# One product per column: TENSOR_TENSOR replaced by TENSOR_SCALAR with a scalar per partition, in the exponential's bias of an attention and feed-forward kernel

## The chip, the core and the metric

The kernel runs on one core of a Trainium2 chip. The metric is the time of one execution in microseconds (us) of the device; lower is better. Engines are named as the profile names them: PE (TensorE, matrix products; its weight loads are PEld), DVE (VectorE), ACT (ScalarE), POOL (GpSimd), SP (the queue from which this kernel starts its DMAs).

## What is computed

Attention with a hash mask, and a feed-forward layer on its result. Cut to what matters:

```
q, k, v: (4, 8, 768, 64);  proj: (64, 6);  w_in: (512, 2048);  w_out: (2048, 512)
q_bucket, k_bucket = 6 sign bits of q @ proj and k @ proj, as a number
scores = where(q_bucket == k_bucket, q @ k.T / 8, -1e9)
attn   = softmax(scores)                       # per row of 768 keys
x      = (attn @ v), heads side by side        # (3072, 512)
h      = x @ w_in
out    = (h * tanh(softplus(h))) @ w_out       # float32, (3072, 512)
```

## The kernel before

The attention is cut into 96 **slots**. A slot takes two heads and 128 queries. Its steps, with the lines of the program:

- **S** (PE, L802): eight matmuls write the scores of both heads into one PSUM tile `ps_s`, 128 x 1536. There is one such tile, so the matmuls of the next slot wait until both exponentials of this slot have read it. The hash codes ride along in the operands, so that a matching pair's score is raised by a large amount.
- **max** (DVE, `scale()`, L809 to L815): a TENSOR_REDUCE (L809) writes the negated maximum of each head's row, two columns, to `svb[:, 0]`. A TENSOR_SCALAR (L812) compares it with a constant and multiplies with a scale per query, which lies in `smalls`: the exponential's scale, `svb[:, 1]`. A TENSOR_TENSOR (L815) multiplies the two: the exponential's bias, `svb[:, 2]`. `svb` and `smalls` lie in SBUF. L812 and L815 come in two versions: both columns in one instruction ("two-wide", 128x2), or each column in its own ("column by column", 128x1 twice).
- **exp** (ACT, L825): one ACTIVATE per head, 128x768, from `ps_s` to `pb` with that head's bias and scale, and the row's sum by the accumulator. When ACT changes its function, an ACT_TABLE_LOAD stands ahead.
- **back**: the sums are made ready (L841 on DVE or POOL, or L838 on ACT), a reciprocal follows (L847, DVE), then the weights are split into a high half (`hl`, L365 on POOL, L367 on ACT or L368 on DVE) and a low half (L386 on DVE, or L392 and L393 on POOL), and DMAs turn them into `PT` (L427).
- **V** (PE, L882): the weights times `v`, into a PSUM tile `ps_t`, which the hash bits and the statistics share (L666, L451, L452; DVE reads them at L670 and L456).

Between the slots stand the feed-forward's matmuls (L913 to L915 with `w_in`, L951 to L953 with `w_out`), ACT's Mish (L931) and its split (L365, L367, L368, L386 on `ffb`), and the preparation of q, k, v and the weights, most of which lies in the first third.

The order of all steps is written out: a list of numbers, `ORDER`, says in which order the steps are issued, and a letter behind a number which version of a step is taken. Every engine works through its own instructions in this order. For the step `max`, 47 slots take the two-wide version and 49 the one column by column. Each of these steps is one version as a whole:

```
op("max", [("DVE", 2200, lambda: scale(False)), ("DVE", 2300, lambda: scale(True))],
   ["ps0", "ps1", f"{sgn}.{j}"], [f"{x}.m0", f"{x}.m1", f"{x}.sc", f"{x}.bi"])
```

Of the kernel before, what the change touches and what calls it, by code (L numbers as in the profile page):

```python
# [15 lines left out]
ALU = mybir.AluOpType  # L16
# [21 lines left out]
class Plan:  # L38
# [3 lines left out]
    def op(self, name, alts, reads=(), writes=(), kind=None, bb=False, after=(), takes=None, frees=None, soft=()):  # L42


        o = Op()
        o.name, o.alts, o.n = name, alts, len(self.ops)
        preds = set(after)
        for regions, write in ((reads, False), (writes, True)):
            for r in regions:
                key, lo, hi = r if isinstance(r, tuple) else (r, 0, 1)  # L50
                for q, a, b, w in self.seen.get(key, ()):
                    if a < hi and lo < b and (w or write) and q is not o:
                        preds.add(q)
        for regions, write in ((reads, False), (writes, True)):
            for r in regions:
                key, lo, hi = r if isinstance(r, tuple) else (r, 0, 1)
                known = self.seen.setdefault(key, [])
                if write:
                    known[:] = [k for k in known if not (lo <= k[1] and k[2] <= hi)]
                known.append((o, lo, hi, write))  # L60
        o.preds = preds
        self.ops.append(o)
        return o
# [173 lines left out]
def lsh_attention_mish_ffn(  # L237
# [10 lines left out]
    nc = tc.nc  # L248
# [18 lines left out]
    op = plan.op  # L267
# [104 lines left out]
    def copied(dst, src, n, engines=("POOL", "ACT", "DVE")):  # L372
# [9 lines left out]
                                                                   op0=ALU.mult)))], [UNIT], [MINUS])  # L382
# [404 lines left out]
    def slot_of(n):  # L787
        u, i = divmod(n, SLOTS)
        j, s = divmod(i, 2)
        return u, u // NU, j, s  # L790

    def att_front(n):

        u, b, j, s = slot_of(n)
        sv, x = svb[:, n % NSV], f"sv{n % NSV}"
        sg, sgn = SIG[u]
        def pe():
            for hh in range(2):
                qi = (2 * j + hh) * 2 + s
                for sl in range(2):  # L800
                    for c0, c1 in ((0, 4), (4, NCH)) if hh == 0 else ((0, 2), (2, NCH)):
                        nc.tensor.matmul(ps_s[:, hh * S + c0 * P:hh * S + c1 * P], QTb[:, u % 2, sl, qi],  # L802
                                         KTb[:, j, sl, hh * NCH + c0:hh * NCH + c1].rearrange("p c t -> p (c t)"),
                                         start=(sl == 0), stop=(sl == 1))
        op(f"S{n}", [("PE", 1300, pe)], [f"QT{u % 2}.0", f"QT{u % 2}.1", f"KT{j}.0", f"KT{j}.1"], ["ps0", "ps1"],
           bb=True)

        def scale(single):
            nc.vector.tensor_reduce(out=sv[:, 0], in_=ps_s.rearrange("p (h e) -> p h e", h=2), axis=AX.X, op=ALU.max,  # L809
                                    negate=True)  # L810
            for w in (slice(0, 1), slice(1, 2)) if single else (slice(0, 2),):
                nc.vector.tensor_scalar(out=sv[:, 1, w], in0=sv[:, 0, w], scalar1=HALF, scalar2=sg[:, j:j + 1],  # L812
                                        op0=ALU.is_le, op1=ALU.mult)
            for w in (slice(0, 1), slice(1, 2)) if single else (slice(0, 2),):
                nc.vector.tensor_tensor(out=sv[:, 2, w], in0=sv[:, 0, w], in1=sv[:, 1, w], op=ALU.mult)  # L815
        op("max", [("DVE", 2200, lambda: scale(False)), ("DVE", 2300, lambda: scale(True))],
           ["ps0", "ps1", f"{sgn}.{j}"], [f"{x}.m0", f"{x}.m1", f"{x}.sc", f"{x}.bi"])

# [275 lines left out]
```

## Time and profile before

| | |
|---|---|
| time, median of 3 runs | 875.53 us (875.09 to 877.47) |
| the profiled execution: its own time, its span | 878.32 us, 876.5 us |
| PE busy | 803.2 us (92%) |
| DVE busy | 695.7 us (79%) |
| ACT busy | 597.0 us (68%) |
| POOL busy | 280.6 us (32%) |

The span reaches from the first instruction to the last. Busy shares are means over the span; the stretches differ. An engine that is idle for most of a stretch can still be the one that the others wait for.

### The profile page before, as it was taken

What the parts mean: (1) busy time and instruction counts of PE and PEld (TensorE: products, weight loads), DVE (VectorE), ACT (ScalarE), POOL (GpSimd) and SP (SyncE); (2) the same over time, 40 slices, a digit from 0 to 9 for tenths busy, and PEclk for the clock granted to TensorE, in tenths of its full rate; (3) what the DMA queues carried; (4) which work ended last, traced back from release to release, by engine and by line L of the source; (5) the groups of instructions that cost most, each with busy time, mean ns of one, the idle gap of its engine ahead of it and who ended that gap; (6) DMA issues with size and microseconds to landing.
All of it is one profiled execution on the core that took longest, in us unless ns stands there. A gap on an engine that the chain in (4) does not pass through costs nothing.

```text
span 876.5 us, 17009 instructions
## 1 busy us (share of the span) xinstructions
PE 803.2 (92%) x6530; PEld 536.5 (61%) x6530; DVE 695.7 (79%) x1344; ACT 597.0 (68%) x947; POOL 280.6 (32%) x260
## 2 busy tenths in 40 slices
PE   2676679899999999999999999999999999999998
PEld 1343347566666767666656766666665766776665
DVE  4697999999899887788889879879888777676412
ACT  5587889878786667668777766567876756657411
POOL 4226443134146433443223212133413143351000
PEclk9697999999999999999999999999999999999999
DMA  9999989589999797688999966899997866556400
GB/s 279 268 243 235 215 195 224 155 187 196 200 172 173 146 186 123 132 156 169 211 188 192 175 122 117 150 178 182 230 161 143 154 120 129 101 98 128 78 25 25
DMA packets 432689, 143.73 MB, mean 164 GB/s; under 512 B 402912, under 2 KB 423392, under 8 KB 432608
## 3 DMA queue, kind: packets, MB, share of 16 engines
q1 hardware_dynamic: 432608, 142.65, 80.9%
q8 instruction: 51, 0.84, 0.4%
q14 instruction: 30, 0.25, 0.1%
HBM read 35.65 MB, written 6.29 MB: 48 GB/s over the span
## 4 chain that ended last, share of the span: by engine, by line
PE 58%; DVE 23%; DMA 8%; ACT 6%; issue 4%; SPq 1%; ACTq 0%; DVEq 0%
PE ps_s L802 10%; PE ps_t L882 8%; DVE svb L809 7%; PE ps_acc L913 7%; PE ps_o L951 6%; PE ps_acc L915 6%; PE ps_acc L914 6%; PE ps_o L953 6%; PE ps_o L952 6%; ACT pb L825 3%; DMA QT<-tok 3%; DVE hl L386 3%; DVE svb L812 1%; DVE ffb L386 1%; DVE svb L815 1%
## 5 line engine op out<-in xcount | busy, mean ns | idle before, releaser
L825 ACT ACTIVATE pb<-ps_s,svb 128x768 f32<-128x768 f32 x192 | 188.8, 986 | 100.9 <-DVE svb L815 84.5
L913 PE MATMUL ps_acc<-X,wi 128*128 128x256 f16 x768 | 209.8, 273 | 0.5 <-ACT ffb L931 0.5
L914 PE MATMUL ps_acc<-X,wi 128*128 128x256 f16 x768 | 209.6, 273 | 0.0
L915 PE MATMUL ps_acc<-X,wi 128*128 128x256 f16 x768 | 209.6, 273 | 0.0
L809 DVE TENSOR_REDUCE svb<-ps_s 128x2 f32<-128x1536 f32 x96 | 168.3, 1753 | 40.6 <-PE ps_s L802 39.4
L386 DVE SCALAR_TENSOR_TENSOR hl<-pb,svb,hl 128x768 f16<-128x768 f32 x146 | 155.8, 1075 | 3.3 <-POOL hl L365 2.7
L802 PE MATMUL ps_s<-KT,QT 128*128 128x512 f16 (+1 forms) x768 | 146.1, 335 | 10.3 <-ACT pb L825 9.7
L953 PE MATMUL ps_o<-wo,ffb 128*128 128x512 f16 x384 | 145.7, 379 | 0.3 <-DVE ffb L386 0.3
L951 PE MATMUL ps_o<-wo,ffb 128*128 128x512 f16 x384 | 145.7, 379 | 0.0
L952 PE MATMUL ps_o<-wo,ffb 128*128 128x512 f16 x384 | 145.7, 379 | 0.0
L365 POOL TENSOR_SCALAR hl<-pb,svb 128x768 f16<-128x768 f32 x66 | 65.3, 990 | 169.8 <-DVE svb L847 73.2
L882 PE MATMUL ps_t<-PT,VT 128*64 128x256 f16 x1728 | 107.6, 280 | 10.9 <-DVE hw L456 4.2
L802 PEld LDWEIGHTS <-QT 128*128 128x128 f16 x768 | 74.2, 99 | 67.2 <-issue 24.1
L882 PEld LDWEIGHTS <-VT 128*64 128x64 f16 x1728 | 94.5, 113 | 29.4 <-issue 23.8
L931 ACT ACTIVATE ffb<-ps_acc,smalls 128x512 f32<-128x512 f32 x96 | 63.5, 684 | 56.0 <-PE ps_acc L915 51.6
L367 ACT ACTIVATE hl<-pb,svb 128x768 f16<-128x768 f32 x77 | 70.9, 929 | 34.1 <-DMA PT<-hl 17.2
L386 DVE SCALAR_TENSOR_TENSOR ffb<-ffb,smalls 128x512 f16<-128x512 f32 x96 | 77.1, 813 | 14.5 <-POOL ffb L365 10.9
L392 POOL TENSOR_SCALAR pb<-pb,svb 128x768 f32<-128x768 f32 x42 | 44.6, 1062 | 136.0 <-ACT hl L367 40.3
L914 PEld LDWEIGHTS <-wi 128*128 128x128 f16 x768 | 75.2, 98 | 14.3 <-issue 1.1
L913 PEld LDWEIGHTS <-wi 128*128 128x128 f16 x768 | 75.1, 98 | 13.1 <-issue 1.4
L915 PEld LDWEIGHTS <-wi 128*128 128x128 f16 x768 | 75.1, 98 | 8.9
L393 POOL TENSOR_TENSOR hl<-pb,hl 128x768 f16<-128x768 f32 x42 | 70.8, 1686 | 3.5
(172 smaller groups left out, 1015.9 us busy)
## 6 DMA issues: line engine op xcount, KB each, us to landing
out_dram<-ffb SPq DMA_DIRECT2D x24, 256.0 KB, 2.8
stg<-in_k_dram SPq DMA_DIRECT2D x12, 384.0 KB, 4.1
stg<-in_v_dram SPq DMA_DIRECT2D x12, 384.0 KB, 4.1
stg<-in_q_dram SPq DMA_DIRECT2D x9, 512.0 KB, 4.9
wi<-in_moe_w_in_dram SPq DMA_DIRECT2D x7, 512.0 KB, 4.9
wo<-in_moe_w_in_dram SPq DMA_DIRECT2D x6, 512.0 KB, 5.1
stg<-in_moe_w_out_dram SPq DMA_DIRECT2D x6, 512.0 KB, 4.7
PT<-hl SPq DMA_TRANSPOSE x192, 4.0
```

The costliest lines, as they stand in the source:

```text
L367: ACT=lambda: nc.scalar.activation(dst, src, AF.Copy, scale=sc),
L386: return [("DVE", 215 + 1.035 * n, port(lambda: nc.vector.scalar_tensor_tensor(out=dst, in0=src, scalar=sc, in1=hi, op0=ALU.mult, op1=ALU. ...
L802: nc.tensor.matmul(ps_s[:, hh * S + c0 * P:hh * S + c1 * P], QTb[:, u % 2, sl, qi], KTb[:, j, sl, hh * NCH + c0:hh * NCH + c1].rearrange(" ...
L809: nc.vector.tensor_reduce(out=sv[:, 0], in_=ps_s.rearrange("p (h e) -> p h e", h=2), axis=AX.X, op=ALU.max, negate=True)
L825: EXP[n, hh] = op("exp", [("ACT", 1075, lambda hh=hh, t=t: nc.scalar.activation(pb[:, t], ps_s[:, hh * S:(hh + 1) * S], AF.Exp, bias=sv[:, ...
L882: nc.tensor.matmul(pv[hh * D:(hh + 1) * D, 0:256], vt[:, w, hh * NCH + c], pt[:, hh, a * NCH + c].rearrange("p s t -> p (s t)"), start=(x ...
L913: nc.tensor.matmul(o, wh, X[:, 0, c], start=(c == 0), stop=False)
L914: nc.tensor.matmul(o, wh, X[:, 1, c], start=False, stop=False)
L915: nc.tensor.matmul(o, wl, X[:, 0, c], start=False, stop=(c == NCC - 1))
L951: nc.tensor.matmul(PS[f"o{s}"], gh, wo[:, g, 0, f2], start=first, stop=False)
L952: nc.tensor.matmul(PS[f"o{s}"], gh, wo[:, g, 1, f2], start=False, stop=False)
L953: nc.tensor.matmul(PS[f"o{s}"], gl, wo[:, g, 0, f2], start=False, stop=last)
```

## The change

In the version column by column, the bias of one column is made by a TENSOR_SCALAR whose tensor operand is the negated maximum and whose scalar operand, one value per partition, is the scale. Before, it was a TENSOR_TENSOR of the two. The two-wide version keeps its TENSOR_TENSOR. The list of the order and the letters in it are unchanged: on every engine the same steps stand in the same places, and on DVE the 98 instructions of the 49 slots column by column are of another kind.

```diff
             for w in (slice(0, 1), slice(1, 2)) if single else (slice(0, 2),):
                 nc.vector.tensor_scalar(out=sv[:, 1, w], in0=sv[:, 0, w], scalar1=HALF, scalar2=sg[:, j:j + 1],
                                         op0=ALU.is_le, op1=ALU.mult)
-            for w in (slice(0, 1), slice(1, 2)) if single else (slice(0, 2),):
-                nc.vector.tensor_tensor(out=sv[:, 2, w], in0=sv[:, 0, w], in1=sv[:, 1, w], op=ALU.mult)
+            if single:
+                for w in range(2):
+                    nc.vector.tensor_scalar(out=sv[:, 2, w:w + 1], in0=sv[:, 0, w:w + 1], scalar1=sv[:, 1, w:w + 1],
+                                            scalar2=None, op0=ALU.mult)
+            else:
+                nc.vector.tensor_tensor(out=sv[:, 2], in0=sv[:, 0], in1=sv[:, 1], op=ALU.mult)
```

## Rows read from the trace of the kernel before

**Rows 1.** Stretches: us, PE, PEld, DVE, ACT, POOL busy (instructions), clock, DMA, GB/s.
```profile
40.00:131.00 91.00, 64.28 (x397) 36.12 (x395) 81.60 (x170) 74.56 (x117) 38.86 (x33) 0.90 0.99 226
131.00:876.50 745.50, 722.67 (x6038) 491.62 (x6038) 591.92 (x1120) 500.99 (x791) 228.75 (x211) 1.00 0.78 151
```

**Rows 2.** Groups by line and shape, DVE: busy us, mean ns | idle before.
```profile
L815 DVE TENSOR_TENSOR svb<-svb 128x1 f32<-128x1 f32 x98 | 26.1, 296 | 0.0
L812 DVE TENSOR_SCALAR svb<-svb,smalls 128x1 f32<-128x1 f32 x98 | 16.4, 209 | 1.7
L812 DVE TENSOR_SCALAR svb<-svb,smalls 128x2 f32<-128x2 f32 x47 | 14.9, 318 | 1.7
...
L841 DVE TENSOR_SCALAR svb<-svb 128x1 f32<-128x1 f32 x60 | 7.3, 147 | 16.4 <-ACT pb L825 16.4
```

**Rows 3.** Timeline, DVE and POOL, three slots: start us, us (joined if touching).
```profile
519.21 1.64 POOL L393 TENSOR_TENSOR hl<-pb,hl 128x768 f16<-128x768 f32 x1
520.84 0.34 DVE L812 TENSOR_SCALAR svb<-svb,smalls 128x1 f32<-128x1 f32 x2
521.09 0.28 DVE L815 TENSOR_TENSOR svb<-svb 128x1 f32<-128x1 f32 x2
...
392.30 1.64 POOL L393 TENSOR_TENSOR hl<-pb,hl 128x768 f16<-128x768 f32 x1
392.84 1.19 DVE L815 TENSOR_TENSOR svb<-svb 128x1 f32<-128x1 f32 x2
...
575.86 0.94 DVE L815 TENSOR_TENSOR svb<-svb 128x1 f32<-128x1 f32 x2
```

**Rows 4.** The chain that ended last, in order of time: start us, us, what.
```profile
41.81 0.92 DVE svb L815 x2
...
82.23 0.54 DVE svb L815 x2
...
89.98 0.20 DVE svb L815 x2
...
96.17 0.62 DVE svb L815 x2
...
149.35 0.53 DVE svb L815 x2
...
254.27 0.80 DVE svb L815 x2
...
392.92 1.11 DVE svb L815 x2
...
777.31 1.03 DVE svb L815 x2
```

**Rows 5.** Timeline of PE at four places: start us, us, [idle before <-releaser].
```profile
254.40 0.38 PE L952 MATMUL ps_o<-wo,ffb 128*128 128x512 f16 x1
254.62 0.38 PE L953 MATMUL ps_o<-wo,ffb 128*128 128x512 f16 x1
255.35 0.18 PE L451 MATMUL ps_t<-smalls,ones 128*128 128x1 bf16 x1 [0.35 <-DVE hsum L670]
...
395.66 0.27 PE L914 MATMUL ps_acc<-X,wi 128*128 128x256 f16 x1
395.77 0.27 PE L915 MATMUL ps_acc<-X,wi 128*128 128x256 f16 x1
396.18 0.38 PE L802 MATMUL ps_s<-KT,QT 128*128 128x512 f16 x1
...
576.29 0.38 PE L953 MATMUL ps_o<-wo,ffb 128*128 128x512 f16 x1
577.07 0.38 PE L882 MATMUL ps_t<-PT,VT 128*64 128x256 f16 x3 [0.40 <-DVE hsum L670]
...
780.11 0.27 PE L915 MATMUL ps_acc<-X,wi 128*128 128x256 f16 x1
780.46 0.38 PE L802 MATMUL ps_s<-KT,QT 128*128 128x512 f16 x1
```

## The prediction

> **What bounds the kernel now.** I read the stretches first [rows 1]. From 131 us to the end PE is busy 722.67 of 745.5 us. All that any change can win there, without touching PE's own work, is the 22.8 us that PE is idle, plus what hides inside PE's modelled ends. From 40 to 131 us it is another picture: PE is busy 64.28 of 91 us and DVE 81.60, so DVE and what hangs on it set the pace, and time won on DVE can become time won.
>
> Then the groups [rows 2]. The column-wise products of L815 take 296 ns in the mean, the column-wise scales of L812, an instruction of the same size with more in it, 209 ns. The timeline says why [rows 3]. At 521.09 POOL's L393 has just ended (519.21 + 1.64 = 520.85), and the two products take 0.28 us together. At 392.84 they take 1.19 us: POOL's L393 began at 392.30 and ends at 393.94, and the products end right behind it, at 394.03. The product stands behind a POOL instruction that began earlier. The reader is to see that no wait on a semaphore shows this; it lies inside the instruction's duration. Where a pair is stretched, a POOL instruction lies across its start or its middle. With some 158 ns as the product's own time (the 0.28 us pair, whose two overlap by some 40 ns, gives about that), the 98 products carry 98 x (296 - 158) = 13.5 us of such waits.
>
> Last the chain that ended last [rows 4], to see which of these waits lie on it. An undisturbed pair shows there with 0.20 us (89.98; the rest of it overlaps the scales). Anything above 0.20 is a wait.
>
> **The change part by part.** *Removed: the wait behind POOL.* The column-wise scale of L812 is already what the product becomes: a TENSOR_SCALAR on one column with a scalar per partition from SBUF. Its mean of 209 ns over 98 instructions, in the very slots in which the product behind it waits, leaves no room for waits of 0.3 to 0.9 us [rows 2]. So I take the wait as gone.
>
> *Added: a dearer instruction.* The new product was not run before. Bounds: 147 ns from below (L841 column-wise, no scalar per partition), 209 ns from above (L812 column-wise, with one) [rows 2]. I take the upper, since the scalar per partition is what the two share. In pairs this is 0.34 us against 0.28 [rows 3], so 0.06 us more per slot; the lower end would make it about nothing. Over 49 slots that is at most 2.9 us of DVE time against 13.5 us of waits removed.
>
> *What of this lies on the path.* I go through the slots on the chain. New pair: 0.20 + 0.06 = 0.26 us.
>
> Before 131 us, where PE has gaps of microseconds, the chain's rows count whole: 82.23 gives 0.54 - 0.26 = 0.28 us, 96.17 gives 0.62 - 0.26 = 0.36 us. In both, DVE's next instruction reads PSUM, so DVE moves up at once. The pair at 41.81 with 0.92 us gives nothing in my sum: DVE's next instruction is a wide TENSOR_SCALAR on SBUF (L368) that I expect to stand behind the same POOL instruction, so that the wait only changes its owner. Four more slots on the chain (at 49, 133, 315 and 466 us) have such a follower, L368 or L386 close behind, and count nothing either.
>
> At 149.35 the chain stays on DVE until long waits of PE some 20 us on: 0.53 - 0.26 = 0.27 us.
>
> After that PE's gap caps what a slot can give, since PE goes on with its own queue. A gap is read from start to start, less the usual step (0.22 us for 512 columns, 0.11 for 256) [rows 5]:
>
> - slot at 254.27: 0.80 - 0.26 = 0.54 us free; PE lost 255.35 - 254.62 - 0.22 = 0.51. Taken: 0.51.
> - slot at 392.92: 1.11 - 0.26 = 0.85 free; PE lost 396.18 - 395.77 - 0.11 = 0.30. Taken: 0.30.
> - slot at 575.86: pair 0.94 against 0.34 [rows 3], 0.60 free; PE lost 577.07 - 576.29 - 0.22 = 0.56. Taken: 0.56.
> - slot at 777.31: 1.03 - 0.26 = 0.77 free; PE lost 780.46 - 780.11 - 0.11 = 0.24. Taken: 0.24.
>
> Sum of the gains: 0.28 + 0.36 + 0.27 + 0.51 + 0.30 + 0.56 + 0.24 = 2.52 us. Against it stand seven column-wise slots on the chain that wait for no POOL instruction, like the one at 89.98: 7 x 0.06 = 0.42 us. The net is 2.1 us off the span, 876.5 to 874.4. All other stalls, the larger part of the 13.5 us, lie where ACT or PE is busy with other work when the bias comes, and that work hides them today: their removal costs and brings nothing.
>
> The profiled execution took 878.32 us, 2.8 more than the median of the runs; I carry the difference over: 875.53 - 2.1 = 873.4 us.
>
> **The rivals.** *More is won than the caps allow.* Exponentials that start earlier bring everything behind them forward, transposes and POOL's halves too, and so also gaps that PE has for other reasons. Without the caps the seven slots give 0.28 + 0.36 + 0.27 + 0.54 + 0.85 + 0.60 + 0.77 = 3.67 us, less 0.42: 3.25, or 872.3 us. If the five slots with a follower that uses POOL's path paid too, at most 0.92 - 0.26 = 0.66 each, it would be 6.5 us, 869.0. For it speaks that DVE is busy 90% from 40 to 131 us; against it, that PE's 722.67 us later leave so little.
>
> *The gain is given back.* PE's gaps are also ended by others (DMAs, ACT's table loads), and a gap that loses one cause can keep its length by the next. Then little is left: 875.5 us. For it speaks that the seven gains are small, 0.24 to 0.56 us, less than one exponential of ACT; against it, that in [rows 5] the releaser at two of four places is DVE's instruction directly behind the pair.
>
> *The change doesn't do what it says: the new product waits too.* For it speaks that a TENSOR_SCALAR can wait: the two-wide L812 takes 318 ns in the mean [rows 2], half as much again as the column-wise one. Against it speaks the column-wise L812 with 209. Then only the price remains, 0.06 us on the some 20 column-wise slots of the chain: 1.2 us, 876.7. The Trainium skill speaks for this rival in its page "SBUF — State Buffer", section "Who interferes with whom": it counts `tensor_scalar` among the operations that can enter a two-port mode and are then shut out while GpSimd works. The same section exempts an instruction with at most one SBUF input outside those modes; by that rule, the trace agrees for one column, with 209 ns.
>
> *Slower: the turn is lost.* Today the short product queues behind POOL and, when it has had its turn, DVE's next instruction follows at once. After the change a long one (L386 or L368 on 768 columns) may ask instead, or start just ahead of POOL's next instruction and hold that one up. Place: the slots whose follower is L386 or L368. Price: POOL's instruction, up to 1.64 us [rows 3], waits for most of one DVE instruction, or the reverse; I take 0.9 us. It decides from six such turns on the path, 5.4 us, which outweigh the 2.1 and add 3.3: 878.8 us. For it speaks that five slots on the chain have such a follower; against it, that the same contest takes place today, one instruction later.
>
> **How the numbers follow.** Chances: forecast 0.50, more is won 0.25, given back 0.10, product waits too 0.07, turn lost 0.08. The runs of this kernel can tell about 0.3%, 2.6 us, from no change: faster means under 872.9 us, slower over 878.2. The forecast's own range is 872 to 875, of which about a quarter (0.12) falls under 872.9. So faster 0.25 + 0.12 = 0.37; slower 0.08 and 0.02 from the run-to-run spread of the others, 0.10; within 0.53. Low end: 870.3, which takes in most of the rival with more gain and leaves out its far end; high end: 876.8, which holds the product that waits too. What is left out is about 0.08 below and 0.09 above.
>
> **What would show it.** The line of the column-wise product should have 98 instructions of about 205 ns, none over 0.3 us, and the DVE instructions behind it should take some of the waits: the means of L368 and L386 on `hl` rise a little. DVE's busy time falls by 5 to 10 us, less than 13.5. PE's waits for the hash sums (L670) near 255 and 577 us vanish. PE's gaps ahead of S that follow two-wide slots stay. The prediction is wrong if the product still shows durations near a microsecond; if the chain's DVE rows vanish but PE's idle time after 131 us doesn't fall by about 1.5 us; or if POOL's durations rise and its halves come late.

## The result and the profile after

The changed kernel takes 870.02 us (median of 13 runs, 868.58 to 874.25) against 875.53 (13 runs): 0.9934 of the time before, 95% interval 0.9921 to 0.9948. That is 5.5 us faster where 2.1 were forecast, and just below the range (870.3). The two profiled executions stand further apart, 868.58 against 878.32 us, than the medians: some of what differs between them is chance, and a second profile of either kernel was taken to tell it apart (below).

The groups by line and shape of VectorE after the change (columns as in [rows 2]). The product is now L816, the two-wide one L819:

```profile
L386 DVE SCALAR_TENSOR_TENSOR hl<-pb,svb,hl 128x768 f16<-128x768 f32 x146 | 157.6, 1088 | 4.3 <-POOL hl L365 3.2 <-ACT hl L367 0.5
...
L368 DVE TENSOR_SCALAR hl<-pb,svb 128x768 f16<-128x768 f32 x49 | 35.7, 728 | 4.5 <-DMA PT<-hl 3.7
...
L812 DVE TENSOR_SCALAR svb<-svb,smalls 128x1 f32<-128x1 f32 x98 | 16.4, 209 | 1.7
L816 DVE TENSOR_SCALAR svb<-svb 128x1 f32<-128x1 f32 x98 | 16.3, 208 | 0.0
```

The product takes 208 ns where it took 296 [rows 2], as much as the scale ahead of it (209): no wait behind POOL is left in it, and its price is the upper bound of the forecast. That it was POOL can be counted: before, 28 of the 98 products take more than 0.25 us, each with a POOL instruction running when it begins; after, 54 of the 98 begin while POOL goes on for at least another 0.15 us, and the longest takes 214 ns. All DVE work together is 8.1 us less (687.6 against 695.7). The product's own line fell from 26.1 to 16.3 us, and L386 and L368 on `hl` took 3.3 us over; their means rose as said (1075 to 1088 and 697 to 728 ns).

PE at the four places of [rows 5], from the timeline after the change (start us, us):

```profile
249.22 0.38 PE L957 MATMUL ps_o<-wo,ffb 128*128 128x512 f16 x1
249.43 0.17 PE L451 MATMUL ps_t<-smalls,ones 128*128 128x1 bf16 x1
...
389.25 0.27 PE L919 MATMUL ps_acc<-X,wi 128*128 128x256 f16 x1
389.36 0.70 PE L802 MATMUL ps_s<-KT,QT 128*128 128x512 f16 x3
...
567.83 0.38 PE L957 MATMUL ps_o<-wo,ffb 128*128 128x512 f16 x1
568.13 0.52 PE L886 MATMUL ps_t<-PT,VT 128*64 128x256 f16 x6
...
770.66 0.27 PE L919 MATMUL ps_acc<-X,wi 128*128 128x256 f16 x1
770.77 0.70 PE L802 MATMUL ps_s<-KT,QT 128*128 128x512 f16 x3
```

Three gaps are gone; at the third place 568.13 - 567.83 - 0.22 = 0.08 us are left of 0.56. These four steps of the forecast came out as written. Most of what was missed lies earlier. This is VectorE and POOL behind slot 8 (slots are numbered from 0; it starts at 94.04 us before), first in the kernel before:

```profile
96.97 1.22 DVE L561 SCALAR_TENSOR_TENSOR wi<-wo,wi 128x1024 int32<-128x1024 int32 x1
98.10 1.40 DVE L368 TENSOR_SCALAR ffb<-ffb,smalls 128x128 f32<-128x128 f32 x1
99.36 1.00 DVE L386 SCALAR_TENSOR_TENSOR hl<-pb,svb,hl 128x768 f16<-128x768 f32 x1
...
98.08 1.34 POOL L546 TENSOR_SCALAR stg<-stg 128x1024 bf16<-128x1024 int16 x1 [1.37 <-ACT pb L825]
```

and in the changed one:

```profile
93.33 0.33 DVE L816 TENSOR_SCALAR svb<-svb 128x1 f32<-128x1 f32 x2
...
93.83 1.21 DVE L561 SCALAR_TENSOR_TENSOR wi<-wo,wi 128x1024 int32<-128x1024 int32 x1
94.96 0.28 DVE L368 TENSOR_SCALAR ffb<-ffb,smalls 128x128 f32<-128x128 f32 x1
95.16 1.01 DVE L386 SCALAR_TENSOR_TENSOR hl<-pb,svb,hl 128x768 f16<-128x768 f32 x1
...
95.32 2.07 POOL L546 TENSOR_SCALAR stg<-stg 128x1024 bf16<-128x1024 int16 x1 [1.37 <-ACT pb L829]
```

Before, L368 began 0.02 us after POOL's L546 and lasted 1.40 us, to POOL's end. After, it begins 0.36 us ahead of L546 and lasts 0.28; the L386 behind it begins ahead of L546 too, by 0.16 us, and now POOL waits, 2.07 against 1.34 us. From L368 to the L386 behind it are 1.26 us before and 0.20 after: 1.06 us, on top of the 0.36 that the pair itself gave. The turn changed hands.

### The profile page after: what moved, and what is told of

Read it like the earlier page. It is cut to its first block, busy times and chain, and to the rows that moved or that the text cites. A ratio compares the mean times of both kernels' runs of the same rounds, so it can differ in the third digit from the quotient of the medians.

```text
span 866.8 us, 17009 instructions
## 1 busy us (share of the span) xinstructions
PE 801.1 (92%) x6530; PEld 534.5 (62%) x6530; DVE 687.6 (79%) x1344; ACT 596.8 (69%) x947; POOL 283.1 (33%) x260
## 4 chain that ended last, share of the span: by engine, by line
PE 65%; DVE 17%; DMA 8%; ACT 5%; issue 3%; POOL 1%; SPq 0%; DVEq 0%; ACTq 0%; POOLq 0%
PE ps_s L802 11%; PE ps_t L886 8%; PE ps_acc L917 8%; PE ps_acc L918 8%; PE ps_acc L919 8%; PE ps_o L955 7%; PE ps_o L957 7%; PE ps_o L956 7%; DVE svb L809 5%; ACT pb L829 3%; DVE hl L386 3%; DMA QT<-tok 2%; DMA PT<-hl 2%; PE ps_l L414 1%; DVE ffb L386 1%
## 5 line engine op out<-in xcount | busy, mean ns | idle before, releaser
L809 DVE TENSOR_REDUCE svb<-ps_s 128x2 f32<-128x1536 f32 x96 | 168.2, 1752 | 41.6 <-PE ps_s L802 40.7
L386 DVE SCALAR_TENSOR_TENSOR hl<-pb,svb,hl 128x768 f16<-128x768 f32 x146 | 157.6, 1088 | 4.3 <-POOL hl L365 3.2
L365 POOL TENSOR_SCALAR hl<-pb,svb 128x768 f16<-128x768 f32 x66 | 64.4, 977 | 169.7 <-DVE svb L851 77.6
L886 PE MATMUL ps_t<-PT,VT 128*64 128x256 f16 x1728 | 105.3, 276 | 7.3 <-DMA PT<-hl 3.7
L886 PEld LDWEIGHTS <-VT 128*64 128x64 f16 x1728 | 92.2, 111 | 25.4 <-issue 20.2
L367 ACT ACTIVATE hl<-pb,svb 128x768 f16<-128x768 f32 x77 | 70.9, 930 | 36.0 <-DMA PT<-hl 17.2
L386 DVE SCALAR_TENSOR_TENSOR ffb<-ffb,smalls 128x512 f16<-128x512 f32 x96 | 78.1, 823 | 15.0 <-POOL ffb L365 11.4
```

The costliest lines, as they stand in the source:

```text
L386: return [("DVE", 215 + 1.035 * n, port(lambda: nc.vector.scalar_tensor_tensor(out=dst, in0=src, scalar=sc, in1=hi, op0=ALU.mult, op1=ALU. ...
L886: nc.tensor.matmul(pv[hh * D:(hh + 1) * D, 0:256], vt[:, w, hh * NCH + c], pt[:, hh, a * NCH + c].rearrange("p s t -> p (s t)"), start=(x ...
```

## The experiments

Each run was timed in turn with the kernel before on the same chip; three were executed once, for a profile. The slot starts that follow are the starts of L809 in each profile. The edits to the changed kernel are conditions on the slot `n`:

```diff
-            if single:
+            if single and CONDITION:          # else the old products
```

**Early and late apart.** Conditions `n <= 12` and `n > 12`.

> The new product only in the ten column-wise slots up to slot 12 (before about 131 us); the old product in the 39 later ones. Theory A (the forecast's sum: only what the chain's rows show is won): 0.6 us from the slots at 82 and 96 us less 0.1 for the price, so 0.5 us less than before, no difference that can be measured. Theory B (the early stretch is bound by VectorE and what hangs on it, so waits there are won with what they trigger; in the two profiles slot 12 starts 5.2 us earlier): 3 to 5 us less than before. Theory C (the two profiled executions differ by chance in the early stretch, where the DMA engines are busy 99%): the start of slot 12 scatters by some us between executions of one kernel, and this run is within 1.5 us of before.

> The new product only in the 39 column-wise slots after slot 12; the old one in the ten early slots. Theory A: the four capped gaps (0.51, 0.30, 0.56, 0.24) and 0.27 at slot 14, less the price, 1.5 us less than before. Theory B: the same or little more, 1.5 to 2.5 us less. Theory D (the later gaps give more than the forecast's caps, as the two profiles say: 4.4 us between slot 12 and the end): 4 us less than before.

Early: 0.9974 (0.996 to 0.9989), 874.53 us; the kernel before, beside these four runs, 875.89. Late: 0.997 (0.9958 to 0.9982), 873.38. So by the ratios the early part is worth 2.3 us (1.0 to 3.5) and the late part 2.6 (1.6 to 3.7). The forecast's sum had 1.5 for the late slots, just below that interval, and 0.5 for the early ones, outside it; theory D's 4 us for the late slots lies outside as well. One of the early kernel's twelve executions, the profiled one, took 2,888 us; it is left out of the ratio (without it the median is 874.24), and the early profile read here is a later one.

**The slots of the sum, and all others.** Conditions `n in (6, 8, 14, 25, 43, 66, 91)` and its opposite.

> The new product only in the seven slots that the forecast's sum counts (6, 8, 14, 25, 43, 66, 91). Theory A: all of the gain and none of the price elsewhere, 2.5 us less than before. Rival: the other slots carry as much (theirs are the five with a follower on POOL's path, and those off the chain), then this has half of the measured 5.5 us or less, and the complement the other half.

> The complement: the new product in the 42 other column-wise slots, the old one in the seven. Theory A: only the price, 0 to 0.4 us more than before. Rival (waits off the chain of before, or in front of a follower that uses POOL's path, pay too): 2 to 3.5 us less than before.

The seven: 0.9964 (0.9949 to 0.998), 872.42 us. The 42 others: 0.9993 (0.9982 to 1.0005), 875.54, no difference. So the forecast chose the right slots. By itself, the relief of 42 slots brings nothing that can be measured, as the forecast said; only the size of the seven was short, 3.2 us against 2.5. Together the two come to 0.43% of the 0.66%; the rest may be spread of the runs or an effect of both together, which these runs can't separate.

**What is chance.** Both kernels once more, and the early one.

> The kernel before once more, for a second profiled execution. Theory C (chance in the early stretch): the start of slot 12 lies 1 to 3 us away from the first one's 131.16. Theory B: it lies within 0.5 us of it, and the first V (near 82.9 us) again runs at half the granted clock and takes 3.4 to 3.5 us. Both: near 445 us PE's wait of 1.1 us for ACT's square of the next tokens is absent (it is absent in all four profiles taken since, of kernels with and without the new product there), so that the span is about 2 us shorter than 876.5.

> The changed kernel once more, for a second profiled execution. Theory B: slot 12 starts at 125 to 127 us again and the first V runs at the full granted clock, 2.2 us. Theory C: slot 12 starts anywhere between 126 and 130 us. Both: the four capped gaps near 247, 389, 567 and 772 us close as in the first profile, so that slots 26, 44, 67 and 92 start 0.5, 0.3, 0.5 and 0.2 us nearer to the slots before them than in the kernel before.

> The new product in the ten slots up to slot 12 only, for a profile of it. Theory B: slot 12 starts as in the changed kernel, 4 to 5 us earlier than in the kernel before, and the steps at slots 26, 44, 67 and 92 are absent. Theory C: slot 12 starts 0.5 to 2 us earlier.

Single executions: 877.06, 872.55 and 871.31 us. The table is worked out from the slot starts of these profiles, of those before and of those on slot 8 below: the time from slot to slot, us.

```
slots from to         8-9    9-12   25-26  43-44  66-67  91-92   start of 12
before                8.30   28.82   7.36   6.95   6.85   6.77   131.16
before, again         8.32   28.78   7.35   6.96   6.86   6.77   129.63
late slots only       8.30   28.81   6.83   6.66   6.38   6.54   131.09
all but the seven     8.31   28.81   7.36   6.95   6.90   6.77   129.59
all but slot 8        8.33   28.85   6.83   6.66   6.38   6.54   130.35
slot 8 held up        8.40   28.87   6.83   6.66   6.38   6.54   129.50
slot 8 only           8.18   27.64   7.36   7.03   6.87   6.78   129.98
the seven             7.48   27.63   6.83   6.66   6.38   6.54   128.41
early slots only      7.22   26.68   7.36   7.08   6.85   6.78   126.06
changed               6.89   27.76   6.83   6.66   6.38   6.54   125.94
changed, again        6.90   27.96   6.83   6.66   6.38   6.54   128.20
```

Two things are to be read here. The four late steps repeat to about a tenth in every profile: where the slot ahead has the new product, 0.53, 0.29, 0.47 and 0.23 us are gone (forecast: 0.51, 0.30, 0.56, 0.24), and elsewhere they aren't. And wherever slot 8 has the new product and isn't held up, the stretch from slot 9 to 12 is 0.9 to 2.1 us shorter and most often also the one from 8 to 9. Theory C is half right: the start of slot 12 scatters by 1.6 us among the kernels with the old product in slot 8 and by 2.3 between the two profiles of the changed one, so of the 5.2 us between the first two profiles a part is chance. Theory B fits the early kernel (slot 12 at 126.06) but not the second profile of the changed one, and that profile shows where most of this scatter sits: the first V, behind slot 6, takes 3.51 us there at a mean granted clock of 0.59, against 2.16 at 1.00 in the first profile, and slot 7 follows slot 6 after 7.70 us instead of 6.19. My guess for the second profile of before was right on the wait near 445 us, which is absent, but wrong on what follows: slot 50 follows slot 48 after 19.40 us there, at a mean granted clock of 0.93, after 19.09 in the first profile, at 1.00, and after 17.7 to 18.9 in the others; the span is 1.2 us shorter, not 2.

**Slot 8 by itself.** Conditions `n == 8` and `n != 8`; and the changed kernel with slot 8 held up ahead of its product:

```diff
+            if n == 8:
+                for w in (slice(0, 1), slice(1, 2), slice(0, 1), slice(1, 2)):
+                    nc.vector.tensor_scalar(out=sv[:, 1, w], in0=sv[:, 0, w], scalar1=HALF, scalar2=sg[:, j:j + 1],
+                                            op0=ALU.is_le, op1=ALU.mult)
             if single:
```

> The new product in slot 8 alone. Theory E (the turn): in the kernel before, VectorE's L368 behind slot 8 asks for POOL's path 0.03 us after POOL's L546 has begun and waits 1.12 us; with the new product it asks 0.35 us ahead and POOL waits instead. Then slot 9 starts 1.2 to 1.4 us nearer to slot 8, of which 0.37 is the product's own wait, and the time is 1.5 to 2.5 us less than before, as PE is also held less at half clock behind it. Theory A (the forecast): 0.36 us, no difference that can be measured.

> The changed kernel with the old product in slot 8. Theory E: slot 9 follows slot 8 as in the kernel before (8.30 us), and the time is 1.5 to 2.5 us more than the changed kernel's 870.0. Theory A: 0.4 us more. If the early gain has other places as well, less than 1 us more.

> The changed kernel; in slot 8 the two column-wise scales are computed three times over, which writes the same values again and holds VectorE up by four issue steps of 0.13 us, 0.52 us in all, ahead of the product. Nothing else differs, and the product still doesn't wait behind POOL. Theory E: L368 now asks 0.15 to 0.2 us after POOL's L546 has begun and waits about a microsecond again, so that slot 9 starts 1.4 to 1.7 us later against slot 8 than in the changed kernel, and the time is 1.5 to 2.5 us more than 870.0. Rival (what is won is the product's own wait, in proportion): slot 9 starts 0.5 us later, and the time can't be told from the changed kernel's.

Slot 8 only: 0.9979 (0.9966 to 0.9991), 874.21 us, by the ratio 1.8 less than before (0.8 to 3.0). All but slot 8: 0.9976 (0.9962 to 0.999), 874.01: of the changed kernel's 0.66%, 0.42% are gone, some 3.7 us (the two intervals together leave 2 to 5), with one pair of products of 49 put back. Slot 8 held up: 0.9996 (0.9979 to 1.0012), 875.76: nothing is left of the gain, though no product waits. The timeline of that kernel at slot 8 (L816 is the repeated scale here, L820 the product):

```profile
94.27 0.58 DVE L816 TENSOR_SCALAR svb<-svb,smalls 128x1 f32<-128x1 f32 x4
94.77 0.33 DVE L820 TENSOR_SCALAR svb<-svb 128x1 f32<-128x1 f32 x2
...
96.41 1.36 DVE L368 TENSOR_SCALAR ffb<-ffb,smalls 128x128 f32<-128x128 f32 x1
...
96.27 1.41 POOL L546 TENSOR_SCALAR stg<-stg 128x1024 bf16<-128x1024 int16 x1 [1.36 <-ACT hl L367]
```

The product takes 0.33 us and waits for nothing; L368 asks 0.14 us after L546 has begun and lasts 1.36 again. Slot 9 starts 8.40 us after slot 8, 1.5 later than in the changed kernel, of which 0.5 is the work added. So what counts at this place is not the product's own wait but which of L368 and L546 begins first. Theory E holds for the turn, with misses in size. With the old product back in slot 8 and with slot 8 held up, slot 9 starts as it said. In the profile of slot 8 alone the turn is won too (L368 0.28 us), but slot 9 starts only 0.1 us nearer instead of 1.2 to 1.4: it waits there for PE (8.18), and the gain shows one stretch later. And the two kernels that lose the turn cost 4.0 and 5.7 us against 870.0, where 1.5 to 2.5 were expected.

That the held-up kernel lost 1.7 us more than all but slot 8 has a place in its profile: from slot 28 to 29 are 8.94 us before, 9.06 and 9.39 in the two profiles of the changed kernel, 9.46 in all but slot 8, and 10.62 here. Up to 9.46 this is a turn lost: L386 on `hl` begins behind a POOL instruction (L365) and lasts 1.33 to 1.52 us, 1.01 before. In the held-up kernel it lasts 1.65, but the larger part is another wait: L386 begins 1.25 us later in its slot than in the changed kernel, with VectorE idle for 0.95 us until ACT's L367, which had itself waited 2.58 us for a DMA.

**More slots column by column.** The two-wide scale still waits behind POOL (L812 two-wide: 310 ns in the mean). Six, then five slots with such waits take the version column by column, all else as in the changed kernel:

```diff
-        op("max", [("DVE", 2200, lambda: scale(False)), ...
+        op("max", [("DVE", 2200, lambda: scale(n in (28, 39, 42, 47, 71, 77))), ...
```

> The changed kernel, and the six two-wide slots whose two-wide scale or product waits behind POOL in the profile (28, 39, 42, 47, 71, 77: 0.4 to 1.4 us each) take the version column by column too. Theory A's way of counting (the wait removed, capped by PE's gap behind it): 0.4 us at slot 39, 0.25 at 42, 0.4 at 71, 0.15 at 77, some at 47, less the price of 0.15 us per slot: 1 us less than the changed kernel, 869. Rival: nothing, since the exponential of these slots is awaited behind other work: 870.

> The changed kernel and the version column by column in five more slots (39, 42, 47, 71, 77), without slot 28, where the run before this lost 0.9 us at the next slot. Steps of 0.45, 0.3, 0.35 and 0.2 us that the profile of the six showed behind 39, 42, 71 and 77 add up to 1.3 us: 868.7 us. Rival: no difference from the changed kernel's 870.0 that can be measured.

Six: 0.994 (0.9921 to 0.9959), 870.08 us. Five: 0.9944 (0.9923 to 0.9964), 871.06. Neither can be told from the changed kernel, so the sums of 869 and 868.7 aren't borne out. One counted step does show: slot 40 follows slot 39 after 6.62 and 6.65 us instead of 7.03 to 7.09 in all others, but steps of this size don't add up to a measurable sum here.

## Why the prediction was wrong

**Right, by the steps.** That the product waits behind POOL and that a TENSOR_SCALAR on one column doesn't (208 ns); the price (0.33 us for a pair, 0.34 assumed); the caps after 131 us, each within 0.09 us; that a wait in front of a follower on POOL's path largely changes its owner (the L368 behind the pair at 41 us takes 1.20 us, 0.74 before); that the slots outside the sum bring nothing (0.9993). Of the two smaller terms, the one at 149 us measures 0.16 us (slot 15 follows slot 14 after 7.98 instead of 8.14) where 0.27 stood, and the one at 82 us can't be read: from slot 6 to 7 the changed kernel's two profiles alone have 6.19 and 7.70 us. PE's idle time from slot 12 to the end fell by 3.4 us in the first pair of profiles and by 1.9 in the second, as the forecast asked (about 1.5). POOL's busy time rose, from 280.6 to 283.1 us, which the forecast had named as a sign against it: POOL now takes some of the waits.

**The step that failed** is the term for the slot at 96 us: "96.17 gives 0.62 - 0.26 = 0.36 us", with the reason that DVE's next instruction reads PSUM and DVE moves up at once. It does, by 0.36 us. But I looked one instruction ahead and not at the fourth, L368, which asked for POOL's path 0.02 us too late. Moved up by 0.36 us it comes first, and 1.06 us more are won: from slot 8 to 9 1.40 us (8.30 to 6.89 and 6.90), four times the term. From slot 9 to 12 another 0.9 to 1.1 us fall away in the changed kernel (28.82 to 27.76 and 27.96). So the term measures 2.3 to 2.5 us in the two profiles of the changed kernel (1.3 in that of slot 8 alone). By the times slot 8 is worth 1.8 us when it alone changes and some 3.7 when it alone is put back, where 0.36 stood. That difference of 1.4 to 3.3 us is the largest part of the 3.4 between 870.0 and 873.4; the late slots may hold another (2.6 us against 1.5).

**The rivals.** The one with more gain named the right side and the wrong cause: the caps held at the four places. Whether exponentials that start earlier brought more elsewhere behind slot 12 isn't shown. The one I put on the slower side, the turn lost, had the cause: the contest of long instructions for POOL's path, one that a short shift decides. I gave it one sign only, and 0.08. It has both, and at the place with the smallest margin it was won. The Trainium skill has a rule for this in "SBUF — State Buffer", section "Who interferes with whom": the order of issue, not the shape of the operation, decides who is blocked. The trace agrees, with the same L368 at 1.40 and at 0.28 us; I had weighed that page for the product alone.

**Left open.** Why the stretch from slot 9 to 12 shrinks as well. Two things differ in it. One is a further turn behind slot 9, where VectorE's L541 and then L368 on `hl` meet a POOL L365, first before, then in the changed kernel:

```profile
106.56 1.64 DVE L541 TENSOR_SCALAR stg<-wi 128x1024 int16<-128x1024 int16 x1
108.10 0.59 DVE L368 TENSOR_SCALAR hl<-pb,svb 128x768 f16<-128x768 f32 x1
...
106.26 1.33 POOL L365 TENSOR_SCALAR wo<-wo 128x1024 f32<-128x1024 f32 x1 [4.70 <-DMA wo<-in_moe_w_in_dram]
```

```profile
102.39 0.74 DVE L541 TENSOR_SCALAR stg<-wi 128x1024 int16<-128x1024 int16 x1
103.02 0.60 DVE L368 TENSOR_SCALAR hl<-pb,svb 128x768 f16<-128x768 f32 x1
...
103.53 1.13 POOL L365 TENSOR_SCALAR wo<-wo 128x1024 f32<-128x1024 f32 x1 [4.40 <-DMA wo<-in_moe_w_in_dram]
```

Before, L541 waits (1.64 us); in the second profile of that kernel L368 does (1.48 us, behind an L541 of 0.74). Slot 10 follows slot 9 after 10.59 and 10.62 us. In both profiles of the changed kernel neither waits, and slot 10 follows after 9.95 and 9.83. But neither waits in the kernel with six more slots either, and there it follows after 10.69. The other thing is one V. Here it is in the kernel before, in the one with slot 8 only, in the one with the early slots only and in the one with five more slots:

```profile
110.85 3.20 PE L882 MATMUL ps_t<-PT,VT 128*64 128x256 f16 x36
```

```profile
110.31 2.15 PE L887 MATMUL ps_t<-PT,VT 128*64 128x256 f16 x36
```

```profile
106.44 2.16 PE L887 MATMUL ps_t<-PT,VT 128*64 128x256 f16 x36
```

```profile
107.57 3.18 PE L886 MATMUL ps_t<-PT,VT 128*64 128x256 f16 x36
```

The same 36 matmuls take 3.20 us at a mean granted clock of 0.66, so in part at the lower of its two levels (1.2 instead of 2.4 GHz), and 2.15 at 1.00. PE had been idle 4.52 us shortly ahead of it before, 2.63 in the changed kernel, yet the second profile of the changed kernel has 2.97 us after the same 2.63. Either thing goes with a shorter stretch without the other: with slot 8 only, L541 waits as before (1.65 us), V is fast and 1.2 us are gone; with five more slots neither L541 nor L368 waits, V is as slow as before (at 0.66) and 0.9 us are gone (27.96). How much each gives in the changed kernel no run separates. Nor is it shown why holding up slot 8 cost more than putting its old product back, beyond the place behind slot 28, nor what the late slots won beyond the 1.7 us of the five steps that can be read.

## What to carry to other kernels

A wait that lies inside an instruction's duration is seen by comparing its mean with that of a like instruction that doesn't wait; a product with one column as a scalar operand, instead of two tensors, took the wait away for 0.06 us per pair. When a step moves up by a few tenths of a microsecond, look for every instruction behind it that contends for the same path within that distance: behind a margin of 0.02 us a term came out at four times its own size here, and behind slot 28 a slot that the change doesn't touch got longer. And caps read from PE's gaps, start to start less the usual step, were good to a tenth of a microsecond at the four places here, where PE is nearly always busy.

## What was not expected of the hardware

One short VectorE instruction can decide microseconds: 0.5 us of repeated work in one slot of 96 took back all of a 5.5 us gain (875.76 against 870.02 us). A TENSOR_SCALAR on two columns still waits behind POOL (310 ns in the mean, single ones over 1.3 us), one on a single column doesn't (208 and 209 ns over 98 each).
